# Whole sums at the end of a fill, a list of their own for the modulation rows, later MLP weight loads, later half-1 v and later v reloads in a fused adaLN attention + MLP kernel

## The chip, the cores and the metric

The kernel runs on one core of one Trainium2 chip. TensorE (PE) multiplies, VectorE (DVE), ScalarE (ACT) and GpSimd (POOL) do elementwise work and reductions, and every transfer between the chip's memories is issued by SyncE (SP), whose instructions are executed one after another. The metric is the device time of one execution in microseconds (us). The kernel is written by a planner: a Python class keeps a model time for each engine, decides in which order instructions are emitted to each engine, and the chip then executes each engine's list in that order, waiting on semaphores where data is not there yet. A wrong estimate in the plan is therefore not an error; it shows as an engine that waits at the head of its list while everything behind it waits too.

## The reference, cut to what matters

The input is x (2048 rows, 512 features), a condition vector c, and weights. The MLP block has a spatial shift between w1 and w2.

```python
mod = (silu(c) @ w_mod).reshape(6, 512)         # sa, ca, ga, sb, cb, gb
h = layernorm(x) * (1 + ca) + sa
q, k, v = split(h @ wqkv)                        # 32 heads of 16
o = softmax(q k^T / 4) v
x = x + ga * (o @ wo)
h = layernorm(x) * (1 + cb) + sb
g = gelu(layernorm(h) @ w1)                      # quarters shifted by +1, -1, +2, -2 rows
h1 = h + shift(g) @ w2
h2 = gelu(layernorm(h1) @ w3) @ w4               # 512 -> 1792 -> 512
x = x + gb * (h1 + h2)
```

All products that feed on weights are made from three partial products (high times high, high times low, low times high), so weights and activations are first split into a rounded part and its remainder.

## The kernel before, in words

**Attention.** Queries are taken in four chunks of 512 rows (quarters of the attention), head pairs in 16 units for each chunk, keys in 16 tiles of 128: 64 units, 1024 steps s of one key tile. For each step and each head of the pair PE makes one score product (`score_part`, tile sc, L956), which ACT turns into a 32-bit integer-coded exponential (L952); 24 steps ahead PE makes the same products the other way round (`max_part`, tile mb, L940) and DVE takes their maximum (L936). The low half of each exponential is made on POOL (`p_low`, L1004) or, where POOL is late by the plan, on ACT (L121). The products with v (`pv_part`, L1026 and L1029) read the v tiles vst, four of them, each holding four key tiles; when the last step of a tile has been multiplied, its reload for the next unit is put on SP's list (`load_v`). The row of shifts that follows from the maxima is written by eight small transfers qtl<-nm on the same SP list.

**The order of the work.** The main loop takes blocks of three half steps. For each block it computes a start from when PSUM banks and exponentials will be ready, lets other work run in the gap before it (`gap`), emits the block, and every second block calls `fill(budget)`. `fill` runs the generators of `sch.gens` in list order, one matmul at a time (`one`), and takes each matmul's cost off a credit: 700 ns for each step in the first quarter (900 ns for its first 32 steps), 500, 500 and 540 ns in the others. One matmul of 512 columns costs 231 ns in the model, so a sum of 12 such matmuls costs 2.8 us and the 2.1 us or 1.5 us of a single `fill` end inside it. A bank that is being summed is `sch.open`; `room()` gives out no second bank while one is open. Attention and the other work share seven PSUM banks.

**What the first quarter fills with.** The list of generators holds `weights_gen` (loads and splits the next weights of q, k, v into one of two buffers wp: `staged` starts a DMA into one of five staging tiles wst and gives back the planned arrival, `split_chain` queues the split on ACT at L425 and DVE at L423), `qkv_gen(0, 3)` (v of head half 0, then v of head half 1) and beside it `qkv_gen(1, 2, 4, 5, 6)` (k and q of the other head groups). `pieces_load` and `pieces_gen` prepare the MLP and output weights: 20 pieces in 40 loads of 256 KB, each through a staging tile, ACT (L843), POOL (L844) and two stores to DRAM (Ws); the 14 loads of w4 and the 4 of wo have one more product on POOL (L833), by the modulation rows gb and ga. These rows come from `mod_gen` (L604 on PE), called inside `pieces_load`: ga ahead of wo, and the rows 3, 4 and 5 (sb, cb, gb) ahead of w4, after every earlier piece has been stored; ga and sb share one tile. Every load of `mod_gen` is followed by a wait until the plan's time of its arrival.

**Drains.** `drain(flag)` steps the plan without attention until a flag is set. The ones that matter here: v of half 1 must be stored 13 steps before unit 8 of the first quarter, and at the end of the first quarter all of v, k, q and "pieces" must be done, because their SBUF space is then given to the MLP stage (`tail`).

**After that.** In each of the quarters 2 to 4 the fill is `tail` of the chunk before (wo, w1, w2, w3, w4 with their norms and gelus, all in sums on the seven banks). The last chunk's tail runs alone after the attention.

The lines that the change touches: `fill` (L198 to L205), `staged` (L406 to L417), `weights_gen` and `qkv_gen` (L784 to L798), `pieces_load` (L802 to L817), `pieces_gen` (L819 to L847), the list of generators (L873), `load_v` and its two calls (L912 and L1037), `sch.add` at L1434 and the start of a block at L1502.

Of the kernel before, what the change touches and what calls it, by code (L numbers as in the profile page):

```python
# [48 lines left out]
DEBT = 3000.0  # L49
CROW, CCOL, CIN, CMID, COUT = 232.0, 230.0, 105.0, 95.0, 95.0  # L50
# [15 lines left out]
WLAT = 4000.0  # L66
WSR = 1
# [10 lines left out]
class Sched:  # L78
# [119 lines left out]
    def fill(self, budget):  # L198
        self.credit = max(min(self.credit, CARRY), -DEBT) + budget
        floor = max(0.0, self.credit - max(BMAX, budget))  # L200
        t = self.T["P"]
        while self.credit > floor and self.one():
            pass
        if self.T["P"] > t:
            self.T["P"] += CFILL  # L205
# [89 lines left out]
def kernel(ctx, tc, A_x, A_wqkv, A_wo, B_w1, B_w2, B_w3, B_w4, c, w_mod, out):  # L295
# [110 lines left out]
    def staged(src3):  # L406

        yield lambda: wst
        t = wst.pop(0)
        f = t.bitcast(F32)  # L410
        o = 0
        n = sum(x.shape[2] for x in src3)
        f3 = f.rearrange("p (k n) -> p k n", n=n)
        for x in src3:
            e = sch.dma(dma.dma_start, f3[:, :, o:o + x.shape[2]], x)
            o += x.shape[2]
        return t, f3, e  # L417
# [366 lines left out]
    def weights_gen():  # L784
        for i, (_, wt, a) in enumerate(todo):
            yield lambda: i <= ready["done"] + (("kq", 0) in done)
            ready[i] = yield from wt(a)
# [5 lines left out]
    def qkv_gen(*ids):  # L793
        for i in ids:
            gen, _, a = todo[i]
            yield lambda: i in ready
            yield from gen(ready.pop(i), a)
            ready["done"] += 1  # L798

    loaded = []  # L800

    def pieces_load():  # L802
        yield lambda: ("v", 0, 2) in done
        for i, (nm, src, nk, n) in enumerate(pieces):
            if i == order["wo"][0]:
                yield lambda: ("vcol", 0) in done and ("vcol", 1) in done
                yield from mod_gen((2, garow, 0.0))
            if i == order["w4"][0]:
                yield lambda: len(wqs) == NWQ and not loaded
                yield from mod_gen((3, sbrow, 0.0), (4, cbrow, 1.0), (5, gbrow, 0.0))  # L810
            src3 = kpn(src)
            for c in range(2):
                yield sch.wait(PLOAD)
                yield lambda: len(wst) > WSR or len(ready) + ready["done"] > len(todo)
                t, _, e = yield from staged([src3[:, c:c + 1] if nk == 2 else src3[:, 2 * c:2 * c + 2]])
                loaded.append((i, nm, c, t, e + WLAT))
        loaded.append(None)  # L817

    def pieces_gen():  # L819
        while True:  # L820
# [18 lines left out]
            def store(i=i, c=c, w=w, f=f, gone=gone):  # L839
                for h, t in enumerate((w.bitcast(F32), f)):  # L840
                    e = sch.dma(dma.dma_start, Ws[i][:, h, 512 * c:512 * c + 512], t)
                sch.after(e, gone)
            sch.chain(*ops, ("A", cA(), lambda f=f, w=w: act.activation(w, f, AF.Copy)),  # L843
                      ("G", cG(), lambda f=f, t=t, w=w: pool.tensor_tensor(t, f, w, op=OP.subtract)),  # L844
                      (None, 0, store), ready=e)
        yield lambda: len(wqs) == NWQ
# [26 lines left out]
    for g in (mod_cols(), bounds(), ln1_T(), qk_first(hi, lo), weights_gen(), qkv_gen(0, 3), qkv_gen(1, 2, 4, 5, 6)):  # L873
        sch.add(g)
# [36 lines left out]

    def load_v(u, i):  # L912

        if u < NU:
# [96 lines left out]
    def pv_part(s, lo):  # L1011
# [3 lines left out]
        if kt == 0 and not lo:  # L1015
            pv[u] = ap_.tile([P, CH], F32, name="pv", tag="v", bufs=1)
        v, acc = vst[kt // 4], pv[u]
# [14 lines left out]
        if lo:  # L1032
# [3 lines left out]
            if kt % 4 == 2:  # L1036
                sch.after(e + 300, partial(load_v, u + 1, kt // 4))  # L1037
# [396 lines left out]
    sch.add(pieces_load(), 0)  # L1434
    sch.add(pieces_gen(), 0)
# [38 lines left out]
    for k, blk in enumerate(blocks + [[]] * (LAG + CPER)):  # L1474
# [24 lines left out]
        for s, i in row:  # L1499
            n += (s >= 0) + (s + LEAD < NS)  # L1500

            start = max(start, banks[n - 1 + 2 * (s < 0)] - t)  # L1502
# [78 lines left out]
```

## Time and profile before

| | |
|---|---|
| three runs | 2115.31, 2119.67, 2126.15 us; median 2119.67 us |
| profiled execution: device time | 2129.35 us |
| its span, first to last instruction | 2127.6 us |
| start of the attention's first step, end of its last | 102.7 us, 1953.5 us |
| first quarter of the attention | 102.7 to 580.2 us |
| unit that follows it | 580.2 to 634.3 us |
| the last tail | 1953.5 to 2127.6 us |

The step times are the starts of the score matmuls (L956), two for each step, in the trace. A unit is 16 steps. In the profile's rows, an instruction group reads line, engine, operation, tile written <- tiles read; idle time of an engine is put down to what ended it. TensorE's matmuls are pipelined: 512 columns show as about 0.39 us each, started 0.235 us apart.

### The profile page before, as it was taken

The page shows a single profiled execution, that of the slowest core. Times are in us where ns is not written, and L with a number is a line of the kernel's source. Part 1 is how long each engine was busy: PE and PEld are TensorE (multiplying, and loading weights), DVE is VectorE, ACT ScalarE, POOL GpSimd, SP SyncE. Part 2 cuts the span into 40 slices and gives each one's busy share as a digit, 9 for nine tenths or more (in the row PEclk, how much of TensorE's full clock was granted, in tenths as well). Part 3 has the DMA queues.
Part 4 walks back from the last instruction along what each step waited for, and adds up shares of the span by engine and source line. Part 5 has one row for each costly group of instructions (what it writes and reads, how often), then busy time and mean ns, then how long its engine had stood idle before and what let it go on. Part 6 is the DMA issues. An engine that isn't in the chain of part 4 may idle for free.

```text
span 2127.6 us, 41619 instructions
## 1 busy us (share of the span) xinstructions
PE 1963.1 (92%) x14464; PEld 1163.4 (55%) x14464; DVE 1648.0 (77%) x2936; ACT 1536.5 (72%) x3320; POOL 1716.3 (81%) x1657
## 2 busy tenths in 40 slices
PE   6979897999859999999999999999989999999899
PEld 4645564554325555555545455555545555555788
DVE  7768686888749887888999888888898878882654
ACT  6367677767846877877868887877768797887353
POOL 4368788878887998988978999989879898998442
PEclk9989998999869998999999999999999999999999
DMA  5786876655573354454633444544534444443432
GB/s 194 187 248 203 222 185 195 177 144 144 144 252 93 88 127 100 136 118 136 155 66 87 108 100 108 138 117 108 172 96 104 108 104 108 112 121 101 176 138 85
DMA packets 228514, 292.69 MB, mean 138 GB/s; under 512 B 121264, under 2 KB 172976, under 8 KB 212016
## 3 DMA queue, kind: packets, MB, share of 16 engines
q1 hardware_dynamic: 228304, 290.02, 50.3%
q8 instruction: 115, 1.88, 0.4%
q14 instruction: 95, 0.78, 0.1%
HBM read 226.49 MB, written 62.91 MB: 136 GB/s over the span
## 4 chain that ended last, share of the span: by engine, by line
PE 58%; ACT 13%; DVE 13%; DMA 5%; POOL 5%; issue 3%; SPq 2%; POOLq 0%; ACTq 0%; DVEq 0%
PE mb L940 12%; PE pv L1029 9%; PE sc L956 9%; DVE mx L936 8%; ACT pt L952 7%; PE w L323 6%; PE w L325 5%; PE w L327 5%; PE pv L1026 4%; POOL pt L1004 2%; SPq L100 2%; DMA kst<-Ks 1%; DMA wst<-in_A_wqkv_dram 1%; PE ot L1056 1%; ACT pt L121 1%
## 5 line engine op out<-in xcount | busy, mean ns | idle before, releaser
L1004 POOL TENSOR_SCALAR pt<-pt 128x1024 f16<-128x1024 uint16 x983 | 1307.4, 1362 | 167.7 <-ACT pt L952 162.9
L936 DVE TENSOR_REDUCE mx<-mb 128x1 f32<-128x512 f32 x2048 | 1280.2, 683 | 209.6 <-PE mb L940 160.7
L952 ACT ACTIVATE pt<-sc 128x512 int32<-128x512 f32 x2048 | 1080.4, 607 | 303.7 <-PE mb L940 243.9
L940 PE MATMUL mb<-kst,qtl 48*128 48x512 f32 x2048 | 766.5, 462 | 90.2 <-ACT pt L952 49.1
L956 PE MATMUL sc<-qtl,kst 64*128 64x512 f32 x2048 | 733.5, 452 | 21.5 <-DMA qtl<-nm 8.8
L940 PEld LDWEIGHTS mb<-kst,qtl 48*128 48x128 f32 x2048 | 354.9, 197 | 302.8 <-ACT pt L952 113.8
L956 PEld LDWEIGHTS sc<-qtl,kst 64*128 64x128 f32 x2048 | 344.1, 190 | 183.3 <-ACT pt L952 55.1
L1029 PE MATMUL pv<-pt,vst 128*32 128x512 f16 x4096 | 366.4, 405 | 0.4 <-DMA vst<-Vs 0.4
L1026 PE MATMUL pv<-pt,vst 128*17 128x512 f16 (+1 forms) x2048 | 215.2, 403 | 0.3 <-ACT pt L121 0.2
L1029 PEld LDWEIGHTS <-vst 128*32 128x32 bf16 x4096 | 92.0, 96 | 164.1 <-issue 107.6
L323 PE MATMUL w<-A,wr 128*128 128x256 f32 (+2 forms) x576 | 176.4, 306 | 1.6 <-ACT A L317 1.4
L325 PE MATMUL w<-A,wr 128*128 128x256 f32 (+2 forms) x576 | 174.2, 302 | 1.1 <-DVE A L313 0.8
L1315 POOL TENSOR_TENSOR g<-xs,g 128x256 fp32r<-128x256 f32 (+2 forms) x144 | 103.4, 721 | 86.0 <-ACT g L1314 85.6
L327 PE MATMUL w<-A,wr 128*128 128x256 f32 (+2 forms) x576 | 172.3, 299 | 0.0
L323 PEld LDWEIGHTS w<-A,wr 128*128 128x128 f32 x576 | 113.4, 197 | 23.9 <-issue 13.9
L325 PEld LDWEIGHTS w<-A,wr 128*128 128x128 f32 x576 | 113.4, 197 | 19.3 <-issue 16.8
L327 PEld LDWEIGHTS w<-A,wr 128*128 128x128 f32 x576 | 113.5, 197 | 12.1 <-issue 12.1
L323 PE MATMUL w<-wr,g 128*128 128x512 f32 x288 | 119.5, 415 | 0.0
L327 PE MATMUL w<-wr,g 128*128 128x512 f32 x288 | 117.8, 409 | 0.3 <-POOL g L1315 0.3
L325 PE MATMUL w<-wr,g 128*128 128x512 f32 x288 | 116.6, 405 | 0.0
L1324 DVE SCALAR_TENSOR_TENSOR sq<-sq,w 128x256 f32<-128x256 f32 (+1 forms) x108 | 43.5, 403 | 80.2 <-ACT xs L1320 73.1
L1330 POOL TENSOR_TENSOR xs<-xs,sq 128x256 f32<-128x256 f32 (+1 forms) x108 | 75.8, 703 | 14.6 <-ACT sq L1329 14.0
(145 smaller groups left out, 2192.2 us busy)
## 6 DMA issues: line engine op xcount, KB each, us to landing
wr<-Ws SPq DMA_DIRECT2D x80, 1024.0 KB, 5.9
vst<-Vs SPq DMA_DIRECT2D x256, 192.0 KB, 2.7
kst<-Ks SPq DMA_DIRECT2D x126, 384.0 KB, 6.7
qtl<-Qs SPq DMA_DIRECT2D x128, 96.0 KB, 5.0
Vs<-vt SPq DMA_DIRECT2D x32, 384.0 KB, 4.8
Ws<-wq SPq DMA_DIRECT2D x40, 256.0 KB, 4.3
Ws<-wst SPq DMA_DIRECT2D x40, 256.0 KB, 4.2
wst<-in_B_w_dram SPq DMA_DIRECT2D x36, 256.0 KB, 4.2
```

The costliest lines, as they stand in the source:

```text
L323: te.matmul(o, lh, rh, start=first, stop=False)
L325: te.matmul(o, lh, rl, start=False, stop=False)
L327: te.matmul(o, ll, rh, start=False, stop=last)
L936: end = sch.crit("D", 605, e + PX, lambda: dve.reduce_max(mxs[u][:, j, g, c:c + 1], b, axis=AX.X))
L940: return ready, lambda: te.matmul(b, lhs, kst[u % 3][r, c * CH:(c + 1) * CH], start=True, stop=True), after
L952: ea = sch.crit("A", 480, e + PX, lambda: act.activation(pt[s][:, j], b, AF.Exp))
L956: return ready, lambda: te.matmul(b, kst[u % 3][r, kt * P:(kt + 1) * P], qst[u][r], start=True, stop=True), after
L1004: e_low[s] = XP["G"] + sch.crit("G", 1345, ready, lambda: pool.tensor_scalar(o, i, 0.5, 1.0, op0=OP.mult, op1=OP.mult))
L1026: te.matmul(acc[r:r + n, :], v[:, (kt + i) % 4, c - n:c].bitcast(F16), pt[s + i].bitcast(F16)[:, j, 0::2], start=False, stop=kt == NKT - 2 ...
L1029: te.matmul(acc[r:r + 32, :], v[:, kt % 4, r:r + 32], pt[s].bitcast(F16)[:, j, 1::2], start=kt == 0, stop=False, skip_group_check=True)
L1315: ("G", cG(n), lambda: pool.tensor_tensor(lo, xs, hi, op=OP.subtract)), (None, 0, end))
L1330: ("G", cG(n), lambda: pool.tensor_tensor(xs, xs, sq, op=OP.mult)), *tail_ops, bank=b)
```

## The change

- `fill` begins new work only while the credit is more than 1000 ns above its floor, and goes on down to 1500 ns below the floor while a bank is open; so a fill mostly ends with a whole sum.
- `staged` gives back an arrival 4000 ns later, for every user: the weights of q, k and v and the modulation rows too. The pieces had that already; theirs stays as it was.
- `weights_gen`: the weights i are loaded when product i-2 is finished (before: when enough products had finished).
- `qkv_gen(0)` alone, and `qkv_gen(1, 2, 3, 4, 5, 6)`: v of half 1 follows the second k group and comes before the third one, in one list.
- `mod_rows` is a generator of its own from the end of the first filled k group on: ga, gb, cb, and sb after all of wo is stored. `pieces_load` starts after the second filled k group (before: when three quarters of v of half 0 were stored), its wo waits for ga, its w4 for gb, and no longer for empty buffers.
- `load_v`: the reload of a v tile is put on SP's list 5000 ns (before: 300 ns) after the tile's last use in the plan, at the latest ahead of its first use.
- The start of a block ahead of step 0 takes an earlier bank where the later one is not free in the plan.

```diff
+START, OVER = 1000, 1500
+VLATE = 5000.0
@@ fill
-        while self.credit > floor and self.one():
+        while self.credit > (floor - OVER if self.open else floor + START) and self.one():
             pass
@@ staged
-        return t, f3, e
+        return t, f3, e + WLAT
@@ weights_gen
-            yield lambda: i <= ready["done"] + (("kq", 0) in done)
+            yield lambda: i < 1 or (("kq", 0) in done if i == 1 else ("todo", i - 2) in done)
@@ qkv_gen
             ready["done"] += 1
+            done.add(("todo", i))
+    def mod_rows():
+        yield lambda: ("kq", 1) in done
+        yield from mod_gen((2, garow, 0.0))
+        done.add("garow")
+        yield from mod_gen((5, gbrow, 0.0))
+        done.add("gbrow")
+        yield from mod_gen((4, cbrow, 1.0))
+        yield lambda: all(("wo", 2 * i + c) in done for i in order["wo"] for c in range(2))
+        yield from mod_gen((3, sbrow, 0.0))
+        done.add("mods")
@@ pieces_load
-        yield lambda: ("v", 0, 2) in done
+        yield lambda: ("kq", 2) in done
         for i, (nm, src, nk, n) in enumerate(pieces):
             if i == order["wo"][0]:
-                yield lambda: ("vcol", 0) in done and ("vcol", 1) in done
-                yield from mod_gen((2, garow, 0.0))
+                yield lambda: ("vcol", 0) in done and ("vcol", 1) in done and "garow" in done
             if i == order["w4"][0]:
-                yield lambda: len(wqs) == NWQ and not loaded
-                yield from mod_gen((3, sbrow, 0.0), (4, cbrow, 1.0), (5, gbrow, 0.0))
+                yield lambda: "gbrow" in done
...
-                loaded.append((i, nm, c, t, e + WLAT))
+                loaded.append((i, nm, c, t, e))
@@ pieces_gen
                 sch.after(e, gone)
+                done.add((nm, 2 * i + c))
...
-        yield lambda: len(wqs) == NWQ
+        yield lambda: len(wqs) == NWQ and "mods" in done
@@ the list of generators
-    for g in (..., weights_gen(), qkv_gen(0, 3), qkv_gen(1, 2, 4, 5, 6)):
+    for g in (..., weights_gen(), qkv_gen(0), qkv_gen(1, 2, 3, 4, 5, 6)):
@@ load_v, pv_part
+    vnext = set()
-        if u < NU:
+        if (u, i) in vnext or not u:
+            vnext.discard((u, i))
             sch.dma(dma.dma_start, vst[i], Vs[units[u][1], :, 4 * i:4 * i + 4])
+        load_v(u, kt // 4) if (u, kt // 4) in vnext else None
...
-                sch.after(e + 300, partial(load_v, u + 1, kt // 4))
+                if u + 1 < NU:
+                    vnext.add((u + 1, kt // 4))
+                sch.after(e + VLATE, partial(load_v, u + 1, kt // 4))
@@ before the main loop
     sch.add(pieces_load(), 0)
+    sch.add(mod_rows(), 0)
     sch.add(pieces_gen(), 0)
@@ start of a block
-            start = max(start, banks[n - 1 + 2 * (s < 0)] - t)
+            free = banks[n - 1 + 2 * (s < 0)]
+            start = max(start, (free if free < LATE else banks[n - 1]) - t)
```

More of the change, by code (lines that the diff above doesn't have):

```diff
@@ L837, in gone, with store @@
                 wqs.append(w)
-            def store(i=i, c=c, w=w, f=f, gone=gone):
+            def store(i=i, c=c, w=w, f=f, gone=gone, nm=nm):
                 for h, t in enumerate((w.bitcast(F32), f)):
@@ L872 @@
                                                   op=OP.subtract)))], mark("w0"), ready=arr["w0"])
-    for g in (mod_cols(), bounds(), ln1_T(), qk_first(hi, lo), weights_gen(), qkv_gen(0, 3), qkv_gen(1, 2, 4, 5, 6)):
+    for g in (mod_cols(), bounds(), ln1_T(), qk_first(hi, lo), weights_gen(), qkv_gen(0), qkv_gen(1, 2, 3, 4, 5, 6)):
         sch.add(g)
```

## The prediction

> **What bounds the kernel now.** I read the page first, for the balance of the engines and for stretches where TensorE falls off.
>
> ```profile
> PE 1963.1 (92%) x14464; PEld 1163.4 (55%) x14464; DVE 1648.0 (77%) x2936; ACT 1536.5 (72%) x3320; POOL 1716.3 (81%) x1657
> PE   6979897999859999999999999999989999999899
> PEclk9989998999869998999999999999999999999999
> ```
>
> PE is nearly always at work, so what other engines save is worth nothing unless PE waits for them. The exceptions are few and sit in the first third: slices 6, 11 and 12, where the granted clock drops too. The stretches by quarter (cut at the first score matmul of a quarter) say the same.
>
> ```profile
> 102.72:580.16 477.44, 431.66 (x3255) 242.28 (x3255) 369.20 (x639) 345.46 (x710) 390.92 (x334) 0.95 0.68 185
> 580.16:634.28 54.12, 26.54 (x188) 13.31 (x186) 22.60 (x39) 27.55 (x54) 48.10 (x40) 0.68 0.77 248
> 1054.54:1502.52 447.98, 430.07 (x3306) 240.18 (x3305) 379.58 (x668) 352.88 (x763) 399.64 (x381) 0.97 0.43 105
> ```
>
> Columns are length, then busy time of PE, PEld, DVE, ACT, POOL, granted clock, DMA. A full quarter of attention takes 448 us with PE idle for 18; the first takes 477 with 46 idle, and the one unit behind it 54 us with 27.6 idle. So some 28 + 28 us are lost around the first quarter, and the change rewrites just that quarter's order. The timeline, at PE's long gaps, names them.
>
> The largest:
>
> ```profile
> 600.54 1.26 POOL L833 TENSOR_TENSOR wst<-wst,gbrow 128x512 f32<-128x512 f32 x1
> 601.83 0.63 ACT L843 ACTIVATE wq<-wst 128x512 fp32r<-128x512 f32 x1 [2.59 <-POOL wst L833]
> 602.54 1.26 POOL L844 TENSOR_TENSOR wst<-wst,wq 128x512 fp32r<-128x512 f32 x1 [0.74 <-ACT wq L843]
> 603.76 1.26 POOL L833 TENSOR_TENSOR wst<-wst,gbrow 128x512 f32<-128x512 f32 x1
> 609.44 0.79 PE L940 MATMUL mb<-kst,qtl 48*128 48x512 f32 x1 [24.65 <-ACT pt L952]
> ```
>
> This is the drain of "pieces" at the quarter's end: w4 loads one behind another, 3.22 us each (603.76 - 600.54), while PE does nothing for 24.65 us. Why so many are left shows in the windows of L844, which each of the 40 loads passes once:
>
> ```profile
> 115.00:259.00 144.00, 22.28 (x17) 0.94 0.79 225
> 259.00:389.00 130.00, 12.39 (x9) 0.93 0.73 198
> 389.00:532.00 143.00, 0.00 (x0) 1.00 0.55 140
> 532.00:584.80 52.80, 6.38 (x5) 0.89 0.57 142
> ```
>
> 17 + 9 + 5 = 31 are done before the drain, 9 in it, and none for 143 us in the middle: there the twelve loads of the rows sb, cb and gb stand ahead of w4.
>
> Three more gaps are waits in the same quarter:
>
> ```profile
> 135.91 0.63 ACT L425 ACTIVATE wp<-wst 128x512 fp32r<-128x512 f32 x1 [6.16 <-DMA wst<-in_A_wqkv_dram]
> 137.08 1.28 PE L940 MATMUL mb<-kst,qtl 48*128 48x512 f32 x2 [8.27 <-ACT pt L952]
> ...
> 259.48 1.86 PE L604 MATMUL mr<-wst,sil 128*128 128x128 f32 x8 [4.07 <-DMA wst<-in_w_mod_dram]
> ...
> 346.58 0.63 ACT L425 ACTIVATE wp<-wst 128x512 fp32r<-128x512 f32 x1 [4.12 <-DMA wst<-in_A_wqkv_dram]
> 348.58 0.63 ACT L425 ACTIVATE wp<-wst 128x512 fp32r<-128x512 f32 x1 [1.38 <-DMA wst<-in_A_wqkv_dram]
> 349.75 1.12 PE L1056 MATMUL ot<-ident,ac 128*128 128x128 f32 x4 [11.16 <-ACT ac L1045]
> ```
>
> At 135.91 and 346.58 ACT stands at the head of its list with a split whose weights have not landed, and the exponentials stand behind it. At 259.48 PE itself does.
>
> **The change, part by part.** The sum is made against the profiled execution, 2129.35 us (span 2127.6 and 1.8 around it), and taken off the median of the runs, 2119.67, which is 0.46% below it.
>
> *Rows in a list of their own, w4 not behind them (drain).* The 24.65 us go if all 40 loads are done before the quarter's end. After the gap PE also runs at a low clock:
>
> ```profile
> 584.79:609.44 24.65, 0.00 (x0) 0.00 (x1) 0.00 (x0) 6.20 (x11) 20.21 (x18) 0.50 0.75 268
> 609.44:612.86 3.42, 3.42 (x16) 2.46 (x20) 2.59 (x5) 3.42 (x8) 3.42 (x4) 0.50 0.86 196
> 612.86:616.27 3.41, 3.41 (x20) 1.73 (x12) 2.91 (x6) 2.91 (x7) 3.41 (x3) 0.73 0.90 183
> ```
>
> 0.50 x 3.42 + 0.27 x 3.41 = 2.6 us, together 27.3. The Trainium skill (TensorE: Matmul & The Clock Gate, "What's actually happening") has the clock halve after an idle window of about 3.4 us and return after as much sustained work; the rows agree in kind. By its figure each of the four gaps over 3.4 us would pay 1.7, 6.8 in all, and the sum below would be 4.2 larger.
>
> Are they done in time? Loads start after the second filled k group instead of at 115. The fill works that group off with its q chunk around 190:
>
> ```profile
> L323 PE MATMUL q<-hT,wp x4: 392/395/398, 184.8 to 189.7; 128*128 128x512 f32 x4
> ```
>
> The order up to there does not change, so say 185. At 144/17 = 8.5 us for each load, 40 need 340: done at 525, against an end of the quarter near 580 - 22 = 558. Four loads in hand. The rows' 16 loads, their matmuls and copies are as many as before; they move to some 125 us on, past the loads of weights on SP's list and into the same fill, one chunk every 12 us (143/12), so gb is there long before w4. So the drain goes, by estimate. The nine loads come back beside attention. What that costs shows in four units without v, k, q in the fill, two before and two with w4 loads:
>
> ```profile
> 485.09:507.96 22.87, 21.77 (x187) 11.07 (x186) 20.95 (x38) 17.89 (x36) 19.86 (x18) 1.00 0.57 152
> 507.96:529.24 21.28, 20.52 (x188) 11.15 (x186) 20.18 (x38) 16.34 (x33) 19.56 (x18) 1.00 0.49 107
> 529.24:554.33 25.09, 22.11 (x171) 9.90 (x167) 21.44 (x37) 20.99 (x43) 22.07 (x19) 0.93 0.46 104
> 554.33:580.16 25.83, 23.12 (x160) 10.16 (x161) 19.25 (x34) 22.24 (x44) 22.97 (x21) 0.87 0.65 172
> ```
>
> 50.92 - 44.15 = 6.8 us for the five, 1.35 each; nothing at the other end, where POOL has room (81% over the span). Nearest to the loads themselves is 1.2: minus 11.
>
> *v of half 1 in one list.* The gap of 11.16 at 338 is its drain: 13 steps before unit 8, its last tiles only just multiplied, then ACT waits for weights. In the new list v follows the second k group alone:
>
> ```profile
> 189.00:338.00 149.00, 29.91 (x192) 25.63 (x192) 6.33 (x15) 10.26 (x31) 0.98 0.76 204
> ```
>
> 192 matmuls in 149 us, 9.3 us for each of 16 tiles, while other k and q groups shared the fill. By the credit a tile of 12 x 0.119 us (the planner's cost) takes 2 steps of 0.7; 16 tiles and the rows 45 steps, so from step 40 to about 85, due at 115. If it kept 9.3 us a tile (5 steps) it would be 5 to 10 steps late and the gap would stay. I take 9 of 0 to 11.
>
> The three parts that are left rest on the list of waits (total us, times, longest):
>
> ```profile
> ACT wp L425 <- DMA wst<-in_A_wqkv_dram: 17.5, 6, 6.2
> PE sc L956 <- DMA qtl<-nm: 8.8, 7, 1.8
> PEld w L325 <- issue: 29.0, 77, 0.8
> PEld w L327 <- issue: 26.4, 73, 0.5
> PEld w L323 <- issue: 24.7, 67, 0.7
> SPq L100 <- PE pv L1026: 704.7, 167, 11.1
> ```
>
> *Arrival 4 us later.* At 136, 6.16 of waiting lose 4.0, and the exponentials get ahead of the split. But v of half 0 is drained at the same place, so of 8.27 I take 4 (0 to 8.3). The 4.07 of the row goes: 4. ACT's other waits at L425, 17.5 - 6.16 - 4.12 - 1.38 = 5.8 us, are worth 3. In the prologue the same 4 us can delay v of half 0, with no attention to cover it: minus 3 (0 to 8).
>
> *v reloads 4.7 us later.* SP stands 704.7 us at reloads whose tile PE still reads, with the shift rows qtl<-nm queued behind; PE waited 8.8 us for those. I take 4. A loss is excluded: a tile is read again 12 steps later, 16 us even at 21.28/16 a step.
>
> *Whole sums.* PE enters a stretch of weight products 217 times (77 + 73 + 67) with its weight load bare, 80.1 us in all, 0.37 each. A sum of twelve wide matmuls that was cut into 7 + 5 now takes one entry. A third fewer entries would be 27 us of PE; but in the stretches that are then longer ACT and DVE run dry, so I take 5, between -10 and +20. The guard at the block start touches only steps before 0: nothing.
>
> Sum: 27.3 - 11 + 9 + 4 + 4 + 3 - 3 + 4 + 5 = 42.3, so 2119.67 - 42.3 = 2077.4 us.
>
> What is late next where the stalls go: POOL. In the first quarter it has 390.9 us in 477; with nine loads of 2.5 us more, and 30 us of span less, (390.9 + 23)/447 = 93%, against 399.6/448 = 89% in the third quarter: it fits, without slack.
>
> **The rivals.** *The loads are late again.* If the 12 us of the rows' chunks set the pace of the staging tiles, 40 loads from 185 end at 661, (661 - 558)/12 = 8 or 9 are left, and 8 x 3.22 + 2.6 = 28.4 come back, less the 9.6 they no longer cost beside attention: 2096. For it: the later start and a fifth user of five tiles. Against it: 17 loads in 144 us while three groups of weights were staged. Where v keeps its slow pace too, 9 more: 2105.
>
> *v alone is late:* 2077 + 9 = 2086.
>
> *Slower: long sums starve ACT.* One 2.5 us sum in the last quarter ends so:
>
> ```profile
> 1837.61 0.50 PE L940 MATMUL mb<-kst,qtl 48*128 48x512 f32 x1
> 1838.18 1.58 ACT L952 ACTIVATE pt<-sc 128x512 int32<-128x512 f32 x3 [1.85 <-PE mb L940]
> ```
>
> ACT idles 1.85 us. A tail has 20 sums of twelve wide matmuls (wo 4, w2 4, w4 12), three quarters 60, the k and q groups 27 more. If each loses 0.7 us for good, 61 us: 2119.67 - 42 + 61 = 2138. It decides from 42.3/87 = 0.49 us a sum. Against it: ACT is busy 79% of the third quarter and has room to catch up, and sums of this length are in a quarter in which PE is busy 96% already.
>
> *Clock.* With nothing to fill, the two units above ran at clock 0.93 and 0.87. If longer attention stretches between sums took the quarters 2 to 4 from the third one's 0.97 to 0.93, its 430 us of PE would grow by 4%, 3 x 18 = 55 us: 2132. The Trainium skill names such a case (the same page, "A second HAM failure mode: psum-queue depth-cycling"): many short idles while cycling through PSUM banks make the clock swing. The third quarter's 0.97 speaks against it.
>
> *Nothing comes of it:* waits move to POOL, which would be the bound at 93%; half of the stalls return, and 2112.
>
> **How the numbers follow.** Forecast 0.60; loads late 0.18; v alone late 0.07; ACT starved 0.05; clock 0.03; nothing 0.07. A measurement of this kernel can tell about 0.5%, 10.6 us: three runs spread over 10.8. Faster by more than that (below 2109): 0.60 + 0.18 + 0.07 less the bad ends of these, 0.83. Slower: 0.08. Within: 0.09. The range goes down by the loads' price (11) and ten more for sums (2056), and up through the late loads with late v (2105).
>
> **What would show it.** Right: no PE gap over 5 us between 150 and 650; the sum of the L844 rows complete before the unit that starts the second quarter, which should take near 26 us instead of 54; first quarter near 455 us; L425's wait for weights under 6 us; fewer bare loads of w on PEld. Wrong: a gap at the quarter's end with L833 and L844 alone at work (late loads); a gap at half of the quarter before ot (v late); a third quarter longer than 448 us, with more of "ACT pt <- PE mb" (sums) or a lower clock in them.

## The result and the profile after

The changed kernel takes 2067.93 us (median of four runs, 2062.65 to 2070.14) against 2120.64 us (2115.31 to 2126.15) for the kernel before: the ratio is 0.9748, with a 95% interval of 0.9716 to 0.9779. Its profiled execution took 2068.17 us, with a span of 2066.2 us.

The page of the changed kernel, first the balance of the engines, then PE and its granted clock in the 40 slices:

```profile
PE 1947.0 (94%) x14464; PEld 1159.2 (56%) x14464; DVE 1638.5 (79%) x2936; ACT 1546.5 (75%) x3358; POOL 1684.5 (82%) x1638
PE   6999989999999999999999999999899999999899
PEclk9999998999999999999989999999999999999899
```

The holes in slices 11 and 12 are gone, and so are those in slices 3, 5 and 7 (the prediction read the one in slice 7, around 350 us, as slice 6); an 8 stands in slice 6 now, and others in slices 29 and 38. The stretches of the changed kernel, cut as before at the first score matmuls (now L972): first quarter, the unit behind it, then quarters 2, 3, 4 and the last tail. The columns are again length, then busy PE, PEld, DVE, ACT, POOL, clock, DMA.

```profile
102.10:566.88 464.78, 436.19 (x3242) 243.31 (x3243) 370.47 (x636) 357.40 (x732) 402.08 (x344) 0.96 0.75 206
566.88:597.17 30.29, 25.45 (x187) 11.91 (x184) 22.59 (x39) 21.00 (x43) 23.85 (x21) 0.89 0.69 211
566.88:1004.46 437.58, 420.01 (x3301) 235.29 (x3297) 371.27 (x667) 350.57 (x785) 387.06 (x383) 0.97 0.48 121
1004.46:1433.94 429.48, 414.96 (x3273) 231.92 (x3272) 374.90 (x667) 354.69 (x770) 390.50 (x379) 0.98 0.47 115
1433.94:1888.20 454.26, 433.26 (x3370) 248.99 (x3369) 353.42 (x632) 356.00 (x783) 395.81 (x386) 0.98 0.45 114
1888.20:2066.20 178.00, 161.35 (x891) 140.38 (x890) 91.90 (x173) 78.61 (x193) 65.78 (x93) 0.96 0.35 132
```

The rows of before that the prediction does not show, quarter 2, quarter 4 and the last tail:

```profile
580.16:1054.54 474.38, 430.24 (x3320) 242.26 (x3319) 377.90 (x670) 356.71 (x792) 417.60 (x408) 0.94 0.50 134
1502.52:1953.96 451.44, 432.93 (x3335) 243.54 (x3334) 354.54 (x629) 356.00 (x780) 403.08 (x392) 0.98 0.43 112
1953.96:2127.57 173.61, 158.60 (x874) 137.55 (x873) 91.45 (x172) 76.72 (x188) 64.10 (x90) 0.97 0.36 135
```

Set against these cuts of before, the 61.4 us between the two spans (2127.6 - 2066.2) come from: prologue 0.6, first quarter 12.7, the unit behind it 23.8, the rest of quarter 2 13.0 (420.26 to 407.29), quarter 3 18.5; and the fourth quarter gives back 2.8, the last tail 4.4. The profiled run of before lies 8.7 us above the median of 2120.64, which is the distance from 61.4 to the 52.7 between the medians.

Not all of this is stalls that went. Quarters 2 and 3 hold 52 matmuls fewer than before (3320 + 3306 against 3301 + 3273), and quarter 4 and the tail 52 more: at 0.235 us each some 12 us were moved behind. And the clock record of the trace, which holds only 0.5 and 1.0, has PE busy at half clock for 132.8 us before and for 109.7 us now, 30.1 and 16.6 of them in quarter 3; matmuls of 256 columns start 0.21 us apart at half clock and 0.12 at full, so by estimate half of the difference, some 11.5 us and 6.8 us, is the clock's share.

How far single profiles scatter shows where two kernels issue the same work: the first quarter took 477.44 us before and 474.25 in e8 below, and attention starts at 102.72, 102.80, 100.17 and 100.47 us in before, e8, e2 and e3, whose lists up to there are the same. A difference of up to 3 us in one stage of two profiles is therefore no reading.

The w4 loads, by the windows of the second POOL step of each load (L844 before, L857 now):

```profile
205.00:350.00 145.00, 20.58 (x16) 0.94 0.81 219
350.00:533.00 183.00, 27.09 (x21) 0.97 0.79 234
533.00:566.88 33.88, 3.88 (x3) 0.99 0.45 111
```

All 40 are through before the quarter ends at 566.88, at some 9 us each (145/16); none is left for a drain. PE's waits over 3 us between 100 and 650 in the timeline of the changed kernel:

```profile
134.26 0.62 PE L1046 MATMUL pv<-pt,vst 128*32 128x512 f16 x4 [3.29 <-DMA vst<-Vs]
...
310.74 2.05 PE L606 MATMUL mr<-wst,sil 128*128 128x128 f32 x8 [4.59 <-DMA wst<-in_w_mod_dram]
...
391.42 0.79 PE L972 MATMUL sc<-qtl,kst 64*128 64x512 f32 x1 [3.56 <-DVE mx L952]
...
588.75 1.04 PE L1046 MATMUL pv<-pt,vst 128*32 128x512 f16 x8 [3.30 <-DMA vst<-Vs]
```

Nothing over 5 us is left. But three of the four are of a kind that before had none of this length: PE waits twice for a reloaded v tile and once for a maximum of DVE. The list of waits of the changed kernel (total us, times, longest):

```profile
PEld w L327 <- issue: 13.6, 38, 0.8
PEld w L325 <- issue: 11.9, 34, 0.5
PEld w L329 <- issue: 10.1, 31, 0.6
PE pv L1046 <- DMA vst<-Vs: 6.6, 2, 3.3
SPq L102 <- PE pv L1043: 494.9, 106, 10.5
```

Bare weight loads at the entry to a sum are down from 217 (80.1 us) to 103 (35.6 us), and SP stands at v reloads for 494.9 us instead of 704.7. ACT's wait for weights at its split (17.5 us before) is this line among the waits of L427:

```profile
  DMA wst<-in_A_wqkv_dram: 1.1, 1
```

### The profile page after: what moved, and what is told of

Same layout as the page of the kernel before. It is cut to its first block, busy times and chain, and to the rows that moved or that the text cites. A ratio compares the mean times of both kernels' runs of the same rounds, so it can differ in the third digit from the quotient of the medians.

```text
span 2066.2 us, 41358 instructions
## 1 busy us (share of the span) xinstructions
PE 1947.0 (94%) x14464; PEld 1159.2 (56%) x14464; DVE 1638.5 (79%) x2936; ACT 1546.5 (75%) x3358; POOL 1684.5 (82%) x1638
## 4 chain that ended last, share of the span: by engine, by line
PE 62%; ACT 15%; DVE 14%; DMA 4%; issue 2%; POOL 1%; SPq 1%; POOLq 0%; DVEq 0%; ACTq 0%
PE mb L956 13%; PE pv L1046 9%; PE sc L972 9%; DVE mx L952 8%; ACT pt L968 8%; PE w L325 6%; PE w L329 6%; PE w L327 5%; PE pv L1043 4%; ACT pt L123 1%; PE ot L1075 1%; DMA vst<-Vs 1%; ACT sq L1338 1%; ACT xs L1339 1%; PE q L325 1%
## 5 line engine op out<-in xcount | busy, mean ns | idle before, releaser
L1020 POOL TENSOR_SCALAR pt<-pt 128x1024 f16<-128x1024 uint16 x964 | 1281.9, 1365 | 141.8 <-ACT pt L968 138.5
L968 ACT ACTIVATE pt<-sc 128x512 int32<-128x512 f32 x2048 | 1083.7, 616 | 253.5 <-PE mb L956 203.7
L956 PE MATMUL mb<-kst,qtl 48*128 48x512 f32 x2048 | 767.3, 459 | 58.7 <-ACT pt L968 25.4
L972 PE MATMUL sc<-qtl,kst 64*128 64x512 f32 x2048 | 729.6, 449 | 11.5 <-DVE mx L952 4.5
L972 PEld LDWEIGHTS sc<-qtl,kst 64*128 64x128 f32 x2048 | 341.3, 188 | 171.9 <-DVE mx L952 57.1
L1043 PE MATMUL pv<-pt,vst 128*25 128x512 f16 (+1 forms) x2048 | 213.5, 399 | 0.5 <-ACT pt L123 0.3
L325 PE MATMUL w<-A,wr 128*128 128x256 f32 (+2 forms) x576 | 176.7, 307 | 1.3 <-ACT A L319 1.1
L327 PE MATMUL w<-A,wr 128*128 128x256 f32 (+2 forms) x576 | 170.3, 296 | 0.9 <-DVE A L315 0.7
L329 PE MATMUL w<-A,wr 128*128 128x256 f32 (+2 forms) x576 | 168.4, 292 | 0.0
L325 PEld LDWEIGHTS w<-A,wr 128*128 128x128 f32 x576 | 111.0, 193 | 30.0 <-DVE mx L952 12.9
L325 PE MATMUL w<-wr,g 128*128 128x512 f32 x288 | 118.8, 413 | 2.1 <-ACT g L1333 1.3
L327 PEld LDWEIGHTS w<-A,wr 128*128 128x128 f32 x576 | 111.1, 193 | 12.7 <-issue 10.4
L329 PE MATMUL w<-wr,g 128*128 128x512 f32 x288 | 115.1, 400 | 0.8 <-POOL g L1334 0.8
L327 PE MATMUL w<-wr,g 128*128 128x512 f32 x288 | 114.6, 398 | 0.0
L329 PEld LDWEIGHTS w<-A,wr 128*128 128x128 f32 x576 | 111.0, 193 | 6.3 <-issue 6.3
L1436 DVE TENSOR_TENSOR x<-x,w 128x512 f32<-128x512 f32 x64 | 44.0, 687 | 88.4 <-PE w L329 88.2
```

The source lines that it names most:

```text
L325: te.matmul(o, lh, rh, start=first, stop=False)
L327: te.matmul(o, lh, rl, start=False, stop=False)
L329: te.matmul(o, ll, rh, start=False, stop=last)
L956: return ready, lambda: te.matmul(b, lhs, kst[u % 3][r, c * CH:(c + 1) * CH], start=True, stop=True), after
L968: ea = sch.crit("A", 480, e + PX, lambda: act.activation(pt[s][:, j], b, AF.Exp))
L972: return ready, lambda: te.matmul(b, kst[u % 3][r, kt * P:(kt + 1) * P], qst[u][r], start=True, stop=True), after
```

## The experiments

Theory 1 is the forecast's: the drain, the arrival and v carry the change, and whole sums are small. The first four kernels took parts alone. Each ratio is to the kernel before on the same chip.

### e1: whole sums alone

```diff
 (kernel before)
+START, OVER = 1000, 1500
-        while self.credit > floor and self.one():
+        while self.credit > (floor - OVER if self.open else floor + START) and self.one():
 (and the changed start of a block ahead of step 0)
```

> The kernel before with the new rule of the fill alone (start over 1000 ns of credit, go on to 1500 below the floor while a bank is open) and the guard at the block start. Theory 1 (the gain of quarters 2 and 3 is that of whole sums): those two quarters lose some 20 to 27 us, quarter 4 and the last tail give part of it back, the drain at the end of the first quarter stays at about 25 us; 2120 - 13 = 2107 us. Rival (whole sums are worth nothing, as the bound of +-5 us in the forecast had it; later reloads of v did it): 2115 to 2125 us, quarters 2 and 3 as before.

Measured: 2078.36 us (2076.23 to 2080.37), ratio 0.979 (0.9765 to 0.9814). Not 5 us but some 44. It gained in every later quarter (436.94 us in the third, 438.61 in the fourth), and it also removed the drain at the first quarter's end, though w4 still waited behind all twelve row chunks. The windows of the loads' second POOL step in e1, whose stretch from 389 to 532 had none before:

```profile
389.00:532.00 143.00, 6.54 (x5) 0.98 0.59 157
532.00:580.23 48.23, 7.77 (x7) 0.85 0.57 168
580.23:590.00 9.77, 3.75 (x3) 0.66 0.85 254
```

The last row chunk was multiplied at 480.5 instead of 526.3, so five loads came 50 us sooner, three were left instead of nine, and PE did not stop for them. The first reading, that the drain belongs to the rows' list, was too narrow: here the rows came through sooner without that list, and the drain went as well. So did the 11.16 us at half of the quarter: the unit from step 112 on took 31.8 us instead of 44.6, with v in its old place.

### e2: later v reloads alone

```diff
 (kernel before)
+VLATE = 5000.0
-                sch.after(e + 300, partial(load_v, u + 1, kt // 4))
+                sch.after(e + VLATE, partial(load_v, u + 1, kt // 4))
 (with vnext, as in the change)
```

> The kernel before with the later reloads of v alone. Theory 1: 2120 - 4 = 2116 us, PE's waits for the shift rows (8.8 us before) mostly gone, quarters 2 and 3 within 5 us of before. Rival (the reloads made the gain of quarters 2 and 3): 2090 to 2095 us.

Measured: 2101.71 us (2095.99 to 2104.32), ratio 0.9896 (0.9868 to 0.9925). The gain is again partly the drain: the long gap at the quarter's end shrank from 24.65 to 14.79 us, the unit from 54.1 to 43.4, while the v drain at half of the quarter stayed (12.69 us). SP's list of waits in e2:

```profile
SPq L101 <- PE pv L1031: 435.1, 100, 10.3
```

270 us less at the head of the one list on which the loads and stores of the pieces also stand. That this is how the part pays was not tested. Neither theory holds: quarters 2 (without its first unit) and 3 fell by 6.9 and 6.5 us, more than the 5 allowed and less than the rival's gain.

### e3: the rows' own list alone

```diff
 (kernel before)
+    def mod_rows(): ...
             if i == order["w4"][0]:
-                yield lambda: len(wqs) == NWQ and not loaded
-                yield from mod_gen((3, sbrow, 0.0), (4, cbrow, 1.0), (5, gbrow, 0.0))
+                yield lambda: "gbrow" in done
 (pieces' start, v's order and the arrival stay as before)
```

> The kernel before with the modulation rows in a list of their own, gb second, w4 waiting for gb alone; the loads start where they did before, v keeps its place. Theory 1: the drain at the end of the first quarter goes (24.65 us and 2.6 us of low clock), up to 11 us come back beside the attention: 2095 to 2104 us. Rival (the drain goes only with the later start and the other order of v): nine loads or nearly as many are still left at the quarter's end, 2115 us or more.

Measured: 2094.51 us (2090.24 to 2101.77), ratio 0.987 (0.9832 to 0.9907). The unit behind the quarter fell from 54.1 to 25.4 us, as the forecast said of this part:

```profile
575.85:601.27 25.42, 23.48 (x187) 11.85 (x185) 22.40 (x39) 20.85 (x43) 23.17 (x20) 0.93 0.76 229
```

The gap of 11.16 us at half of the quarter went here too, with v in its old place: the unit from step 112 on took 27.5 us. In exchange PE stood at row chunks that had not landed, 10.10 us at 125 and 3.73 at 216.

### e4: the changed kernel with v's second half beside the k and q groups

```diff
 (changed kernel)
-    for g in (..., weights_gen(), qkv_gen(0), qkv_gen(1, 2, 3, 4, 5, 6)):
+    for g in (..., weights_gen(), qkv_gen(0, 3), qkv_gen(1, 2, 4, 5, 6)):
```

> The changed kernel with v of half 1 back in the list of v of half 0, beside the k groups. Theory 1 (the serial place of v makes its drain 13 steps before unit 8 late: that unit took 51.8 us of the changed kernel's first quarter): the unit falls under 40 us and the time to about 2068 - 8 = 2060 us. Rival (the fill's work there has to be done at some time anyway, and the serial order pays elsewhere): 2068 us or more.

Measured: 2064.38 us (2059.8 to 2067.52), ratio 0.9722 (0.9695 to 0.9749): not to be told from the changed kernel. The first quarter was 18 us shorter (446.44): the unit from step 112 on fell from 51.8 to 31.4 us, as theory 1 said, with no v matmul left in it. But the drain at the quarter's end came back, as the timeline of e4 shows:

```profile
570.43 0.79 PE L956 MATMUL mb<-kst,qtl 48*128 48x512 f32 x1 [14.56 <-ACT pt L968]
```

So the serial order is not what removes v's gap: without it, beside whole sums and the late start of the loads, the gap stays away and the pieces' drain returns.

### e5: the changed kernel without whole sums

The parts alone gave 2.1, 1.04 and 1.3%, all of it 2.5%. Theory 2: whole sums carry most, some 25 us of it in the later quarters, and the other parts remove the same drain. The rival: on top of the others they are small.

```diff
 (changed kernel)
-        while self.credit > (floor - OVER if self.open else floor + START) and self.one():
+        while self.credit > floor and self.one():
```

> The changed kernel with the old rule of the fill (new work down to the floor, stop there). Theory 2 (whole sums are worth some 25 us from the second unit of quarter 2 on, with or without the other parts; in quarter 1 the rows' list does what they would do): 2068 + 25 = 2093 us, that stretch near 1490 us of the 1469 in the changed kernel. Rival (the later v reloads give the same, and the two only replace each other): 2068 to 2078 us.

Measured: 2071.72 us (2070.39 to 2076.12), ratio 0.9763 (0.972 to 0.9805), not to be told from the changed kernel. The sum of theory 2 fell, though its stretch did grow: from the second unit of quarter 2 on it is 1484.6 us here and 1469.0 in the changed kernel. The time lies where the rival put it, but not for the rival's reason, as the windows of e5 (first quarter, then quarters 2 to 4) show:

```profile
98.38:554.46 456.08, 430.66 (x3252) 239.98 (x3253) 368.75 (x637) 354.44 (x728) 408.56 (x347) 0.97 0.75 211
...
554.46:1001.83 447.37, 426.17 (x3321) 239.31 (x3317) 376.40 (x671) 349.69 (x781) 393.06 (x389) 0.97 0.49 125
1001.83:1440.26 438.43, 422.77 (x3284) 235.11 (x3283) 377.68 (x667) 350.60 (x761) 398.18 (x381) 0.98 0.44 106
1440.26:1893.99 453.73, 435.86 (x3358) 246.62 (x3357) 355.43 (x630) 357.36 (x782) 402.29 (x391) 0.98 0.44 114
```

Against these, whole sums in the changed kernel gain 9.8 us in quarter 2 and 8.9 in quarter 3, and lose 3.7 in the prologue (start at 98.38, not 102.10), 8.7 in the first quarter and 2.5 in the last tail. Two windows name the place of the loss, the unit from step 112 on, ahead of which v's second half is due; the changed kernel first, then e5:

```profile
296.44:348.22 51.78, 43.60 (x276) 28.28 (x272) 27.03 (x48) 30.29 (x66) 37.42 (x35) 0.84 0.90 260
```

```profile
305.51:338.04 32.53, 29.41 (x195) 15.86 (x192) 23.58 (x41) 23.76 (x49) 29.14 (x25) 0.90 0.83 243
```

The (x) behind PE counts matmuls: 81 more in the changed kernel, 60 of them of v, which e5 had behind it. With whole sums the plan reaches the due time with five v tiles not yet multiplied and does them while attention stands. Another 16 of the 81 are of a modulation row, whose chunk PE waits for in this unit (the 4.59 us at 310). Whole sums alone do not make v late: e1 and e4 have them too, and no v matmul in this unit.

### e6: the changed kernel with early reloads

```diff
 (changed kernel)
-VLATE = 5000.0
+VLATE = 300.0
```

> The changed kernel with the v reloads 300 ns after the last use in the plan, as before the change. Theory 2: beside whole sums the later reloads add little: 2068 to 2074 us, and SP's waits for the v products go back up to about 650 us of 495. Rival (they keep the 22 us that they were worth alone): 2085 to 2090 us.

Measured: 2075.6 us (2066.44 to 2079.1), ratio 0.9769 (0.9727 to 0.9811). The interval overlaps the changed kernel's, so the later reload's share is not settled by the times. SP's waits went back up to 636.4 us, as expected. In the profile the first quarter is 11.7 us longer than the changed kernel's (476.46 against 464.78), but the four runs spread over 12.7 us and the profiled one is the slowest of them. Quarters 2 to 4 take 439.27 + 436.80 + 440.93 = 1317.0 us here and 437.58 + 429.48 + 454.26 = 1321.3 with late reloads: from the second quarter on the late reload saves nothing that these profiles can tell.

### e7 and e10: three parts together, then with the arrival

e7 is the kernel before with e1, e2 and e3 in it; e10 adds the arrival.

```diff
 (e7: kernel before with whole sums, mod_rows and late reloads; e10 in addition:)
-        return t, f3, e
+        return t, f3, e + WLAT
-                loaded.append((i, nm, c, t, e + WLAT))
+                loaded.append((i, nm, c, t, e))
```

> The kernel before with three parts of the change: whole sums, the rows' list, later v reloads. Arrival of weights, start of the loads and the place of v as before the change. Theory 2 (what the change adds to these three, the serial v of half 1 and the later start above all, costs as much as it brings in the first quarter): 2055 to 2066 us, at least as fast as the changed kernel, no drain at the quarter's end. Rival (the later arrival and the new order carry part of the gain): 2080 us or more.

> The kernel before with whole sums, the rows' own list, the later reloads of v and, new against e7, the arrival that is planned 4 us later for all weights. Theory: the arrival is what e7 lacked, since it lost 7.43, 3.14, 2.44 and 9.64 us in four gaps of the first quarter and the changed kernel only 4.59 us at a row chunk; then the first quarter falls from 478.2 to about 465 us and the time is 2062 to 2069 us. Rival: the one-after-another order of v and of groups 1 to 6 and the pieces' later start carry it; then the time stays at 2072 to 2078 us.

Measured: e7 2076.16 us (2074.25 to 2078.16), ratio 0.9778 (0.9743 to 0.9813); e10 2067.49 us (2063.92 to 2069.9), ratio 0.9736 (0.9707 to 0.9765). e7 lies between its theory and its rival, so the three parts are not the whole of it. The intervals of e7 and e10 overlap a little, but the profiles agree with the arrival: the first quarter falls from 478.2 to 467.8 us. e7's timeline has PE waiting three times at a row chunk

```profile
139.49 1.83 PE L606 MATMUL mr<-wst,sil 128*128 128x128 f32 x7 [3.14 <-DMA wst<-in_w_mod_dram]
...
278.53 1.62 PE L606 MATMUL mr<-wst,sil 128*128 128x128 f32 x6 [2.44 <-DMA wst<-in_w_mod_dram]
...
355.25 0.98 PE L606 MATMUL mr<-wst,sil 128*128 128x128 f32 x3 [9.64 <-DMA wst<-in_w_mod_dram]
```

and e10's once, beside a wait for v:

```profile
141.24 0.62 PE L1045 MATMUL pv<-pt,vst 128*32 128x512 f16 x4 [8.62 <-DMA vst<-Vs]
...
344.69 1.20 PE L606 MATMUL mr<-wst,sil 128*128 128x128 f32 x4 [6.17 <-DMA wst<-in_w_mod_dram]
```

e10 stands where the changed kernel does (0.9736 and 0.9748). What it lacks, the serial order of v, the later start of the pieces and the new rule for when weights are loaded, is together worth nothing that these runs can tell.

### e8: whole sums from the second quarter on, nothing else

```diff
 (kernel before; sch.whole is False until the first quarter's drains are done)
-        while self.credit > floor and self.one():
+        while self.credit > ((floor - OVER if self.open else floor + START) if self.whole else floor) and self.one():
```

> The kernel before with the new rule of the fill from the end of the first quarter on alone. Theory 2: the first quarter with its drain stays as before (24 to 25 us without PE), the rest from the second unit of quarter 2 on falls from 1493 to about 1467 us: 2120 - 26 = 2094 us. Rival (the gain of whole sums came only through the first quarter, what is after it falls by chance of the planner's order): 2110 us or more.

Measured: 2101.41 us (2099.73 to 2104.28), ratio 0.9899 (0.9863 to 0.9934), between the two theories. Quarter 2 was 9.8 us shorter than before, quarter 3 9.5, quarter 4 12.7, the tail 5.5 longer, and both drains were whole (24.98 us at the end). So of e1's 2.1%, 1.0% is what sums gain in later quarters. By the profiles the other half stands at the first quarter's end, where the next unit took 54.8 us here and 30.0 in e1; the first quarter itself did not get shorter in e1 (474.25 here, 476.05), though the gap at its half went.

### e9: the changed kernel, whole sums from the second quarter on

Theory 3, from e5 and e8: whole sums gain in the later quarters whatever else is done, and cost in the first quarter once its drains are gone.

```diff
 (changed kernel; sch.whole as in e8)
-        while self.credit > (floor - OVER if self.open else floor + START) and self.one():
+        while self.credit > ((floor - OVER if self.open else floor + START) if self.whole else floor) and self.one():
```

> The changed kernel, but lumps stop by the old rule until the end of the first quarter and by whole sums from there on. Theory 3: whole sums gain in quarters 2 and 3 (447.4 to 437.6 us and 438.4 to 429.5 us from the changed kernel without them to the changed kernel) and cost in quarter 1 (456.1 to 464.8 us), where a sum that may not be cut stands in front of attention. Then the quarters here are near 456, 438, 430 and 454 us and the time is some 9 us under the changed kernel's, 2056 to 2062 us. Rival: quarter 1's order under whole sums is what makes quarter 2 short; then quarter 2 stays near 447 us and the time lies at 2067 to 2073 us.

Measured: 2053.41 us (2048.6 to 2054.07), ratio 0.9667 (0.9643 to 0.9691). The interval lies below the changed kernel's and below e5's: theory 3 stands, with 14 us against 9 expected. The windows of e9:

```profile
98.13:554.45 456.32, 430.96 (x3252) 239.89 (x3253) 368.45 (x637) 354.83 (x728) 408.55 (x348) 0.97 0.75 211
...
554.45:990.36 435.91, 418.47 (x3300) 234.59 (x3296) 371.29 (x667) 351.01 (x785) 387.24 (x383) 0.98 0.47 121
990.36:1418.27 427.91, 412.54 (x3275) 230.22 (x3274) 374.46 (x667) 355.06 (x770) 390.85 (x379) 0.99 0.46 116
1418.27:1873.20 454.93, 433.59 (x3370) 248.81 (x3369) 353.25 (x632) 356.09 (x783) 396.01 (x386) 0.98 0.44 114
```

Start and first quarter are e5's (98.38, 456.08), quarters 2 to 4 are those of the changed kernel. e5 and e9 differ in whole sums from quarter 2 on alone, and so price them: quarters 2 to 4 take 1339.5 us in e5 and 1318.8 here, 20.8 less, of which the last tail gives 3.3 back (175.5 and 178.7 us). PE's busy time in quarters 2 to 4 falls by as much, 1284.8 to 1264.6 (20.2), so what goes is not idle time. Three things are in these 20.2. The tail has 17 matmuls more, some 4 us of work that was moved. PE is busy at half clock for 45.6 us instead of 52.3, some 3 us. The rest, some 13 us, goes by estimate with the sums that start anew. The waits of e5, then of e9:

```profile
PEld w L327 <- issue: 28.8, 77, 0.8
PEld w L329 <- issue: 26.7, 73, 0.5
PEld w L325 <- issue: 24.7, 67, 0.5
```

```profile
PEld w L328 <- issue: 14.1, 38, 0.8
PEld w L326 <- issue: 11.8, 33, 0.7
PEld w L330 <- issue: 10.1, 31, 0.7
```

115 bare loads fewer (217 to 102) are 44.2 us less of waiting at them; the 13 us of PE's time make 0.11 us for each, an estimate, since no run changes these entries alone.

### e11 and e12: v beside, pieces early

```diff
 (e11: e4, and)
-        yield lambda: ("kq", 2) in done
+        yield lambda: ("v", 0, 2) in done
 (e12: e11 with e9's rule)
```

> The changed kernel with v's second half beside the groups of k and q, as before, and with the pieces' loads starting after v's first half, as before. Theory: e4 (v beside, late start) had the shortest first quarter, 446.4 us, and gave 14 us back in a drain of 14.56 us at its end (second quarter 451.5 against 437.6 us); an earlier start ends the pieces' loads earlier and removes the drain, so 2064.4 less 12 to 14: 2048 to 2056 us. Rival: earlier pieces share the ring with the first groups' weights and the modulation chunks, and the wait returns there; then 2062 to 2072 us.

> e11 and e9 in one kernel: v beside, pieces early, whole sums only from the second quarter on. If both theories hold and add, some 9 us under e11, 2040 to 2050 us. If both do their work by taking the same waits out of quarter 1, no better than e11: within 4 us of it. If an early start with cut sums brings the drain back, a gap of 10 us or more stands near 570 us and the time is over 2060 us.

Measured: e11 2059.49 us (2058.2 to 2068.27), ratio 0.971 (0.968 to 0.9739); e12 2047.51 us (2046.85 to 2058.24), ratio 0.9656 (0.9624 to 0.9688). In e11 the drain of e4 did go, but the first quarter was 462.74 us long instead of 446.44:

```profile
103.97:566.71 462.74, 432.29 (x3243) 242.10 (x3243) 368.77 (x637) 353.95 (x726) 406.68 (x347) 0.97 0.75 207
566.71:595.98 29.27, 25.46 (x187) 12.11 (x184) 22.50 (x39) 21.04 (x43) 23.61 (x20) 0.88 0.71 218
```

16 us came back in the quarter: among it a wait of 8.79 us for v at 142, one of 5.69 us at a row chunk, and a unit from step 112 that took 55 us. The expected 2048 to 2056 was missed; theory and rival each have a part. e12 is the fastest that was measured, clearly faster than the changed kernel, inside the 2040 to 2050 us of its first theory, and not to be told from e9 (0.9667). Its unit from step 112 on took 44.9 us with 48 v matmuls in it, though sums are cut in that quarter.

## Why the prediction was right, and where its terms were wrong

The forecast was 2077.4 us, the time 2067.93: right in direction and about right in size. The size is in part luck: the terms add up to 42.3 us of the profiled execution, and between the two profiles 61.4 us went, at other places than the sum has them. The terms were right and wrong as follows.

**The drain (27.3).** Right: 23.8 us at that unit, no drain, forty loads through by 551 (forecast 525). The rows' list does it alone (e3). But the credit went too narrowly to it: e1 removed nearly all of this drain without it and e2 a good part, so the parts cannot be added.

**The nine loads beside attention (-11).** They did come back there: POOL went from 390.9 to 402.1 us in the first quarter, 87% of it. Their price was not measured by itself.

**v of half 1 (9).** Failed. The 11.16 us gap is gone, but the unit did not get shorter: 44.6 us before, 51.8 after, with 60 v matmuls multiplied in front of attention. The working took the serial list as enough to have v done in time, by counting steps of credit. It is neither enough nor needed: in the changed kernel five of v's tiles are late, and the gap goes with v in its old place too (e1 31.8 us for the unit, e3 27.5). Taking either whole sums or the serial list out of the changed kernel brings the unit down to 32.5 us (e5) and 31.4 (e4), so it is the two together that make v late there. That is not the only way to make it late: with v beside the other groups and the loads started early, as before, the unit takes 62.2 us in e7, 58.6 in e10, 55.0 in e11 and 44.9 in e12, with 48 to 66 v matmuls in it. What sets v's pace in the plan stays open.

**Arrival (4 + 4 + 3).** The wait that it aims at went from 17.5 to 1.1 us, and from e7 to e10 the span fell by 9.4 us (2075.3 to 2065.9), with the intervals of the runs overlapping a little. Of its places one was wrong: the row chunk's 4.07 us did not go, a chunk is still waited for 4.59 us; and at 130 a wait for v of 3.29 us stands where 8.27 were.

**Prologue (-3).** The attention starts at 102.1 us instead of 102.7. Cut sums start it at 98.1 (e9), so in the changed kernel it is the whole sums that use up the prologue; the other two kernels with the later arrival and cut sums agree (98.4 in e5, 98.3 in e12). That the arrival costs 3 is not shown: e10 starts 2.6 us later than e7, no more than the scatter, and e1, without the later arrival, starts at 104.2.

**v reloads (4, a loss excluded).** Mis-sized and wrong in its exclusion. The shift rows' 8.8 us went to 1.5; alone the part was worth 1.04%, perhaps because the pieces' transfers stand on the same SP list, which was not tested. And PE does wait for late tiles now, 3.29 and 3.30 us; the argument of 12 steps counted from a reload that starts when the plan says so.

**Whole sums (5, -10 to 20).** The net on top of the rest is 3.2 us of span (e5 to the changed kernel), close to the 5, and the runs cannot tell it from nothing; the working was not close, so this is luck. From e5 to the changed kernel quarters 2 to 4 gain 18.2 us (20.8 from e5 to e9), the prologue and the first quarter lose 12.4 and the last tail 2.5, which leaves 3.2. The mechanism priced at 27 us, fewer entries with a bare load, is in it with some 13 us: half of the bare loads went instead of a third, at some 0.11 us of PE each instead of 0.37. The forecast had no term for a loss at a due time.

**Later quarters.** No term existed for what quarters 4 and the tail give back, 7.2 us. It goes with the 52 matmuls that quarters 2 and 3 no longer hold: quarter 4 has 35 of them and the tail 17.

By place, then: first quarter 455 forecast and 464.8 measured, quarters 2 and 3 hardly moved in the forecast and 31.5 us shorter beyond the drained unit, some 12 of them work that was moved. The total came near because the misses point opposite ways, and because the kernel before has its median 8.7 us below its profiled run.

**The rivals.** *Loads late again* and *v alone late* are told apart by the unit rows: the first did not happen, the second did in another form, with PE mostly at work (4.59 us of that unit are a wait for a row chunk). *Long sums starve ACT:* ACT's wait for PE's mb products fell, from 243.9 to 203.7 us. *Clock:* the third quarter's is 0.98 after 0.97; it rose instead of falling. *POOL as the bound:* busy 87% of the first quarter; the 2112 us of that rival do not follow from its own words, since half of 42.3 off 2119.67 is 2098.5.

**Left open.** Why the 14.3 us between e9 and the changed kernel exceed the 12.4 us lost up to the first quarter's end: 3.2 of the rest lie in quarters 2 and 3, which run the same rule, and the fourth quarter and the tail differ by 1.4 the other way. The clock can be all of that: in quarters 2 and 3 e9 spends 30.7 us at half clock and the changed kernel 41.0. Where exactly the late reload pays in the changed kernel was not settled either (e6's interval overlaps). Kernels with the late arrival, the serial place of v, the later start of the loads or the rule for loading weights as their only edit were not run.

## What to carry to other kernels

Letting filler work end with a whole product paid here in the stages that have slack; ahead of a hard due time it cost in one kernel (e9 against the changed kernel) and removed a stall in another (e1 against e8). So measure such a rule by stage and switch it by stage, since one stage's loss can hide the other stage's gain (e5 and e9). Parts of a change that remove the same drain do not add up: before adding terms, ask of each whether another one would already have removed the stall. And price a late item by what the plan would still have to do at its due time, not by the gap alone; a drain that keeps the engine busy shows no gap, mostly more instructions in a unit.

## What was not expected of the hardware

With fewer starts of sums PE's busy time fell and not its idle time: 20.2 us, some 13 of them beyond moved work and clock, for 115 bare weight loads fewer, while length less busy time stays (54.7 and 54.2 us in quarters 2 to 4 of e5 and e9). The reloads of v tiles take longer from issue to landing when they are put on the list later, 4.9 us median instead of 2.7 (4.6 in e2 with that edit alone, 2.7 again in e6 without it), though SP stands before them less; why was not tried. The row of the DMA issues, before and changed:

```profile
vst<-Vs SPq DMA_DIRECT2D x256, 192.0 KB, 2.7
```

```profile
vst<-Vs SPq DMA_DIRECT2D x256, 192.0 KB, 4.9
```

And a gap of 4.59 us in the middle of the first quarter is followed by a low clock as in the drain before; the windows of the changed kernel around its end at 310.7 (busy times as above):

```profile
309.00:313.00 4.00, 2.26 (x10) 2.29 (x11) 0.92 (x3) 2.01 (x5) 2.34 (x3) 0.50 1.08 361
313.00:317.00 4.00, 4.00 (x26) 3.75 (x25) 0.54 (x2) 1.55 (x5) 0.29 (x1) 0.72 1.15 332
```

The clock is 0.50 around the gap's end and 0.72 over the next 4 us; the record itself has half clock from 308.4 to 315.2 us and full clock behind it, so the 0.72 is an average over the switch. The Trainium skill (TensorE: Matmul & The Clock Gate, "What's actually happening") has the clock halve after an idle window of some 3.4 us and return with sustained work; these rows agree in kind. They do not agree on a whole idle window: the gap begins at 306.2, 2.2 us before the clock halves, and PE was busy for 1.2 of the 3.4 us up to that point.
